# Weight units during attention: fixed steps behind the bias additions in place of every sixth slot

## The chip, the cores and the metric

The kernel runs on one core of one Trainium2 chip. The metric is the device time of one execution in microseconds (us). Five engines work side by side, each on its own queue and in the order of that queue: TensorE (PE, with its weight loads listed as PEld), VectorE (DVE), ScalarE (ACT), GpSimd (POOL) and SyncE (SP, which here only issues DMAs).

## The reference

Attention with a bias made by a small network, and behind it two feed-forward blocks, all in float32:

```python
# q, k, v: (4, 8, 576, 64); hidden 32
scores = scale * np.matmul(q, k.transpose(0, 1, 3, 2))
x = (psi_rel / psi_i)[..., None]           # log distances of positions
bias = np.maximum(x @ w1 + b1, 0.0) @ w2   # per head, the same for every batch
scores = scores + bias - max;  attn = exp(scores) / sum;  out = attn @ v
# 2304 tokens, 512 wide
h = x @ w_in                               # 512 x 2048
g = h * np.clip(h + 3.0, 0.0, 6.0) / 6.0
x = g @ w_out                              # 2048 x 512
gate = 1 / (1 + np.exp(-(x @ w_gate)));  val = x @ w_val    # 512 x 1536
y = (gate * val) @ w_out2                  # 1536 x 512
```

## The kernel before

A short first stage computes the bias and stores it in DRAM (about 57 us). Attention follows (to about 335 us), then the first feed-forward block (to about 750 us) and the second (to the end).

**Attention.** Two heads of one batch make a head unit; there are 16 (`NU`), numbered 0 to 15 here, and each is cut into nine steps (`NSTEP`), 0 to 8. Two steps in a row make a slot (`slot_of_two`, line 463), so an even head unit begins with a slot of its own, and an odd one shares its step 0 with step 8 of the unit before. A step is: score matmuls into a PSUM tile `s`, of which there are two (`scores`, line 342); the bias addition with a row minimum on DVE (line 346); the exponential on ACT, which also writes the row sum into `stat` (line 362); transposes of the probabilities on PE (line 400), copied out of PSUM by DVE or ACT (lines 390 and 392); and, some slots later, the products with v (lines 432 and 435) and their scaling on DVE (line 444). After steps 5 and 8 `invert` adds a constant to the row sums (line 368) and takes the reciprocal (line 369) on DVE. The q and k of the next head unit are split into a high and a low part by `prep`, in the main on POOL (lines 314 and 318); this work can begin when the last scores of the head unit before have been computed, since it overwrites their buffers.

**Weight units.** The weights of the feed-forward blocks come as 64-bit words and are turned into a high and a low float32 part, one block of 128 x 512 at a time: a weight unit. One weight unit is a DMA of the raw words (line 159, SP), an absolute value (line 175, ACT), a clamp (line 176, DVE), a shift (line 184, DVE), two merges with the raw words (lines 186 and 188, DVE), a rounding copy (line 192, ACT) and a subtraction (line 193, POOL). There are two buffers for raw words and three for the work tile `z`, each taken in the order in which the program asks for them. Ten weight units (`NPRE`) are made during attention by `whole`, which issues all eight instructions of a unit at the end of every sixth slot from slot 12 on (slots 12, 18, ... 66). Weight units 10 and 11 are begun by `tick` in slots 70 and 73 (`PRIME`), and the rest during the feed-forward blocks.

**What sets the order.** A scheduler orders each engine's queue ahead of time by a planned time for each instruction: whatever is ready goes in the order in which the program was written, and an instruction written later goes ahead when nothing written earlier is ready. `tc.issue_after(x)` adds an edge: what is written inside it for the engine of `x` is queued behind `x`, without a wait for its end; instructions for other engines are free. Before the change, the weight units stand behind `last_v`, the latest load of v, a DMA of SP: so their raw DMAs are queued behind it, and their DVE, ACT and POOL instructions are free. `PRIME`'s ticks have no such edge.

Of the kernel before, what the change touches and what calls it, by code (L numbers as in the profile page):

```python
# [10 lines left out]
F32 = mybir.dt.float32  # L11
F32R = mybir.dt.float32r
I32 = mybir.dt.int32
AF = mybir.ActivationFunctionType
ALU = mybir.AluOpType
# [3 lines left out]
P = 128  # L19
# [6 lines left out]
NSTEP = 9  # L26
# [18 lines left out]


NPRE = 10
EVERY = 6
PRIME = (NU * NSTEP // 2 - 2, NU * NSTEP // 2 + 1)
NALL = 19  # L50

# [45 lines left out]
def block_kernel(ctx: ExitStack, tc: tile.TileContext, q, k, v, mlp, w_in, w_out, w_gate, w_val, w_out2, dist_d,  # L97
                 rows_d, out):
    nc = tc.nc
# [24 lines left out]
    def ring(name):  # L124

        if name == "z":
            return stg.tile([P, 512], F32, name="z", bufs=3)
        return stg.tile([P, 2, 512], F32, name="raw", bufs=2)

    class Loader:  # L130
# [22 lines left out]
        def dma(self, i):  # L153
            if i < len(self.units) and self.units[i][1] is not None and i not in self.sent:
# [4 lines left out]
                nc.sync.dma_start(raw, self.units[i][1].bitcast(I32))  # L159
                self.sent.add(i)  # L160

        def magnitude(self, i):
            if i in self.raw:
                kind, _, to = self.units[i]
                raw = self.raw[i]
                if kind == "corner":
                    q, e, gv = to
                    if (e, gv) == (0, 0):
                        self.Z = moe.tile([P, 4, 2, 2 * P], F32, name="corners")
                    z = self.Z[:, 2 * e : 2 * e + 2, gv]  # L170
                    raw = raw.rearrange("p (k f) w -> p k f w", k=2)
                else:
                    z = ring("z")
                self.z[i] = (z, raw)
                nc.scalar.activation(z, raw[..., 1].bitcast(F32), AF.Abs)
                nc.vector.tensor_scalar(out=z, in0=z, scalar1=2.0**-15, scalar2=None, op0=ALU.max)

        def assemble(self, i):
            if i not in self.raw:
                return  # L180
            self.raw.pop(i)
            z, raw = self.z[i]
            zi = z.bitcast(I32)
            nc.vector.tensor_scalar(out=zi, in0=zi, scalar1=3, scalar2=0x3FFFFFF8, op0=ALU.logical_shift_left,
                                    op1=ALU.bitwise_and)
            nc.vector.scalar_tensor_tensor(out=zi, in0=raw[..., 1], scalar=-0x40000000, in1=zi,  # L186
                                           op0=ALU.bitwise_and, op1=ALU.bitwise_or)
            nc.vector.scalar_tensor_tensor(out=zi, in0=raw[..., 0], scalar=29, in1=zi,
                                           op0=ALU.logical_shift_right, op1=ALU.bitwise_or)

        def halve(self, z, slot, eng):
            nc.scalar.copy(slot[:, 0], z)  # L192
# [5 lines left out]
        def stage(self, z, idx):  # L198
            hl = self.pair()
            self.halve(z, hl, nc.gpsimd)  # L200
            nc.sync.dma_start(w_d[idx], hl.bitcast(F32))
            self.staged.add(idx)
# [23 lines left out]
                self.mix(to[1], to[2])  # L226
            self.done = i + 1

        def whole(self):
            i = self.n  # L230
            for stage in (self.dma, self.magnitude, self.assemble):
                stage(i)
            self.finish(i, nc.gpsimd)
            self.n += 1

        def tick(self):
            i = self.n
# [24 lines left out]
    load = Loader()  # L262

    attn = ExitStack()
    apool = attn.enter_context(tc.tile_pool(name="apool", bufs=1))
# [11 lines left out]
    Ks = [apool.tile([P, 2, 2, S], F32R, name=f"k{i}") for i in range(2)]  # L277
    Pm = [apool.tile([P, S + 64], F32, name=f"pm{i}") for i in range(2)]
    ident = apool.tile([P, P], F32, name="ident")
    stat = apool.tile([P, 5, NSTEP], F32, name="stat")  # L280
    low, sums = [stat[:, i] for i in range(2)], [stat[:, i] for i in range(2, 5)]
    spread = apool.tile([P, 5 * P], F32, name="spread")
    inv = apool.tile([P, S], F32, name="inv")
    w1c, b1c, w2bd = mlpc[:, 0:1], mlpc[:, 1:3], mlpc[:, 3:35]
# [44 lines left out]
    pts, us, avs, last_u, last_s = {}, {}, {}, [None], [None]  # L329
# [119 lines left out]
    last_v = [None]  # L449
# [3 lines left out]
    for n in range(NU):  # L453
        i = (NSTEP * n + 5) // 2 + 2
# [51 lines left out]
    with ExitStack():  # L506
# [20 lines left out]
        for i in range(2):  # L527
# [5 lines left out]
                                op1=ALU.mult)  # L533
# [30 lines left out]
        for G in range(NG):  # L564
            hid = [hids[(4 * G + ct) % 12] for ct in range(4)]
            nd = max(S - 16 * G, 16 * G + 16)
            for ct in range(4):
# [3 lines left out]
                else:  # L571
                    nc.vector.tensor_scalar(out=hid[ct][:, 0:nd], in0=tbl[:, 0:nd], scalar1=bpsi[:, 1, qd : qd + 1],  # L572
                                            scalar2=None, op0=ALU.max)
# [23 lines left out]
        def split_x(t, cs=range(4)):  # L597
            for c in cs:
                XH, XL = XS[t % 2][:, 0, c], XS[t % 2][:, 1, c]
                nc.scalar.copy(XH, tok(t)[c])  # L600
                eng = nc.gpsimd if 1 in XS else nc.vector
                eng.tensor_tensor(out=XL, in0=tok(t)[c], in1=XH.bitcast(F32), op=ALU.subtract)
# [21 lines left out]
        for i in range(NSLOT):  # L624
            slot_of_two(i)
            if i == NS // 2:
                w = keep.tile([P, 8 * TW], F32R, name="early")
                XS[0] = w.rearrange("p (r c t) -> p r c t", r=2, c=4)
                split_x(0)
            if i in (NS // 2 + 1, NS // 2 + 2):  # L630
                f = len(begun)
                begun[f] = hardswish(ring("z")[:, 0:TW], project(0, slots[2 * f], pp.tile([P, 2, 512], F32, name="s")[:, 0]))
            if i % EVERY == 0 and i > 10 and load.n < NPRE:
                with tc.issue_after(last_v[0].ins):
                    load.whole()
            if i in PRIME:
                load.tick()

        attn.close()
        moe = ctx.enter_context(tc.tile_pool(name="moe", bufs=1, reuse_waits="tile"))  # L640
# [225 lines left out]
        for v, (p, j) in enumerate(visits):  # L866
# [9 lines left out]
            for n in range(2):  # L876
                t = 2 * j + n
                os = bank(n)[0:NB]
                sums = [fp.tile([P, DM], F32, name="sum", bufs=4) for _ in range(NB)]
# [46 lines left out]
```

## Time and profile before

| | us |
|---|---|
| median of 3 runs | 1159.1 (1158.35 to 1160.71) |
| the profiled execution: its own time | 1160.52 |
| the profiled execution: its span in the trace | 1158.7 |
| PE busy | 1135.9 (98%) |
| DVE busy | 772.8 (67%) |
| ACT busy | 588.4 (51%) |
| POOL busy | 422.6 (36%) |

The span is the time from the first instruction to the last one's end. A busy share is an average over the stages. A matmul's end is modelled in the trace, so gaps on PE below some tenths of a microsecond are not seen in its busy time, and the length of a repeated stretch says more.

### The profile page before, as it was taken

To read this page: it belongs to the slowest core of one execution; us is meant where nothing else is said; L and a number is where in the kernel's file an instruction comes from. 1 tells how busy PE (TensorE), PEld (TensorE's weight loads), DVE (VectorE), ACT (ScalarE), POOL (GpSimd) and SP (SyncE) were. 2 spreads that over 40 slices of the span, in tenths; PEclk is the share of its full clock that TensorE was granted. 3 is DMA by queue.
4 is the path that set the end of the run, shared out by engine and by line. 5 is a ranking of instruction groups with operands and counts; after the bars stand their busy time and mean duration, and the time that the engine had idled before them with its cause. 6 is when DMAs were issued, how large, how long until landed. Compare 5 with 4: busy or idle time off the path is not lost.

```text
span 1158.7 us, 19146 instructions
## 1 busy us (share of the span) xinstructions
PE 1135.9 (98%) x6862; PEld 1012.2 (87%) x6862; DVE 772.8 (67%) x1495; ACT 588.4 (51%) x1296; POOL 422.6 (36%) x342
## 2 busy tenths in 40 slices
PE   8799999999999999999999999999999999999998
PEld 3277777777779999999999999999899898998997
DVE  8977878788868887355386775585367655644443
ACT  7988887877855545454455454342333222221221
POOL 0154544544316433232347445261333223311211
PEclk9999999999999999999999999999999999999999
DMA  6854436353213665249467759976878848757532
GB/s 203 298 162 110 158 95 183 112 165 103 78 55 110 209 218 200 101 174 340 167 228 255 253 189 357 395 261 251 308 254 309 311 165 299 285 181 258 191 109 73
DMA packets 83183, 236.82 MB, mean 204 GB/s; under 512 B 9616, under 2 KB 12304, under 8 KB 83088
## 3 DMA queue, kind: packets, MB, share of 16 engines
q1 hardware_dynamic: 83088, 235.60, 58.6%
q8 instruction: 54, 0.88, 0.3%
q14 instruction: 41, 0.34, 0.1%
HBM read 154.15 MB, written 81.41 MB: 203 GB/s over the span
## 4 chain that ended last, share of the span: by engine, by line
PE 84%; DVE 6%; ACT 2%; DMA 2%; issue 1%; POOL 1%; SPq 0%; POOLq 0%; DVEq 0%; ACTq 0%
PE o L673 17%; PE h L807 10%; PE o L807 10%; PE s L342 6%; PE o L862 6%; PE h L862 5%; PE h L611 5%; PE h L610 5%; PE h L612 5%; PE av L432 5%; PE tr L400 4%; PE av L435 1%; DVE z L186 1%; DVE u L346 1%; PE tr L379 1%
## 5 line engine op out<-in xcount | busy, mean ns | idle before, releaser
L673 PE MATMUL o<-gh,slot 128*128 128x384 f32 x768 | 196.0, 336 | 1.8 <-DVE take L392 1.8
L673 PEld LDWEIGHTS o<-gh,slot 128*128 128x128 f32 x768 | 139.2, 188 | 2.3 <-DVE take L392 2.1
L673 PE MATMUL o<-gl,slot 128*128 128x384 f32 x384 | 129.1, 336 | 0.7 <-DVE gl L659 0.7
L362 ACT ACTIVATE p<-u,stat 128x576 f32<-128x576 f32 x128 | 98.7, 773 | 29.2 <-DVE stat L346 28.4
L342 PE MATMUL s<-k,q 128*128 128x288 f32 x640 | 111.0, 309 | 0.7 <-ACT ptm L557 0.4
L346 DVE CUSTOM_DVE_ANT_0 u<-s,bias 128x576 f32<-128x576 f32 x128 | 93.6, 753 | 24.4 <-PE s L342 23.2
L843 POOL TENSOR_TENSOR gp<-s,gp 128x384 fp32r<-128x384 f32 x36 | 39.4, 1107 | 177.0 <-ACT gp L842 92.6
L617 DVE SCALAR_TENSOR_TENSOR g<-g,h 128x384 f32<-128x384 f32 x94 | 51.6, 549 | 70.2 <-ACT g L616 70.1
L659 DVE TENSOR_TENSOR gl<-g,gh 128x384 fp32r<-128x384 f32 x94 | 63.1, 671 | 48.3 <-ACT gh L658 45.8
L658 ACT CAST gh<-g 128x384 fp32r<-128x384 f32 x94 | 48.3, 513 | 91.6 <-DVE g L617 91.3
L193 POOL TENSOR_TENSOR hl<-corners,hl 128x512 fp32r<-128x512 f32 x42 | 57.2, 1366 | 94.3 <-ACT hl L192 79.3
L342 PEld LDWEIGHTS s<-k,q 128*128 128x128 f32 x640 | 88.8, 189 | 2.3 <-ACT ptm L557 0.6
L616 ACT ACTIVATE g<-h,half 128x384 f32<-128x384 f32 x94 | 54.3, 578 | 58.4 <-PE h L612 57.9
L807 PE MATMUL o<-x,slot 128*128 128x384 f32 x432 | 78.4, 336 | 1.4 <-DVE sum L787 1.4
L432 PE MATMUL av<-ptm,vn 128*64 128x288 f32 x512 | 77.8, 419 | 0.7 <-DVE x L444 0.7
L807 PE MATMUL h<-x,slot 128*128 128x384 f32 x432 | 77.8, 335 | 0.0
L807 PEld LDWEIGHTS o<-x,slot 128*128 128x128 f32 x432 | 75.1, 188 | 2.0 <-DVE sum L787 1.7
L807 PEld LDWEIGHTS h<-x,slot 128*128 128x128 f32 x432 | 75.2, 188 | 0.7
L400 PE MATMUL tr<-ident,p 128*128 128x128 f32 x512 | 72.2, 275 | 2.2 <-ACT inv L390 1.5
L673 PEld LDWEIGHTS o<-gl,slot 128*128 128x128 f32 x384 | 72.5, 189 | 1.3 <-DVE gl L659 1.3
L314 POOL TENSOR_TENSOR k<-early,one 128x576 fp32r<-128x576 f32 x30 | 34.4, 1167 | 106.3 <-DVE x L572 53.1
L843 POOL TENSOR_TENSOR x<-s,x 128x384 fp32r<-128x384 f32 x36 | 40.3, 1129 | 84.2 <-ACT x L842 50.5
(157 smaller groups left out, 2725.2 us busy)
## 6 DMA issues: line engine op xcount, KB each, us to landing
w<-hl SPq DMA_DIRECT2D x67, 512.0 KB, 3.3
slot<-w SPq DMA_DIRECT2D x67, 512.0 KB, 5.8
raw<-in_part_dram SPq DMA_DIRECT2D x50, 512.0 KB, 4.1
x<-xc SPq DMA_DIRECT2D x56, 384.0 KB, 6.0
sum<-sum SPq DMA_DIRECT2D x72, 256.0 KB, 3.5
early<-xc SPq DMA_DIRECT2D x28, 384.0 KB, 6.4
nbias<-ptm SPq DMA_DIRECT2D x36, 295.5 KB, 3.1
early<-in_part_dram SPq DMA_DIRECT2D x32, 288.0 KB, 4.3
```

The source lines that it names most:

```text
L342: last_s[0] = nc.tensor.matmul(ps[:, a, 0:HS], Q[:, q0 : q0 + P], K[:, r, h, HS * a : HS * a + HS], start=(i == 0), stop=(i == len(mm) - 1))
L346: last_u[0] = nc.vector.tensor_tensor_reduce(out=halves(u), in0=ps[:, :, 0:HS], in1=halves(bt), op0=ALU.add, op1=ALU.min, scale=-0.125, sc ...
L362: nc.scalar.activation(probs(t), us.pop(t), AF.Exp, bias=low[n % 2][:, s : s + 1], scale=-1.0, accum_out=sums[n % 3][:, s : s + 1])
L400: nc.tensor.transpose(ps[:, kc], pts[n, c][:, h, 64 * h + P * kc : 64 * h + P * kc + P], ident)
L432: nc.tensor.matmul(ps[64 * h : 64 * h + 64, 0:HS], vt[:, 4 * h + g], ptm[:, h, g, cols], start=(g == 0), stop=False)
L610: nc.tensor.matmul(ps[:, 0:TW], wh, XH[:, c], start=(c == 0), stop=False)
L611: nc.tensor.matmul(ps[:, 0:TW], wl, XH[:, c], start=False, stop=False)
L659: last_g[0] = nc.vector.tensor_tensor(out=gl, in0=g, in1=gh.bitcast(F32), op=ALU.subtract)
L673: nc.tensor.matmul(os[c][:, 0:TW], sl[:, r, P * c : P * c + P], x, start=(first and r == 0 and x is gh), stop=(last and x is gl))
L807: nc.tensor.matmul(ps[b], sl[:, r, o : o + P], x[:, c, s], start=(k < 4 and i == 0), stop=(i == len(mm) - 1), skip_group_check=True)
L843: nc.gpsimd.tensor_tensor(out=G[:, i, 1], in0=s, in1=G[:, i, 0].bitcast(F32), op=ALU.subtract)
L862: nc.tensor.matmul(os[i], x[:, P * i : P * i + P], slots[(base + 14 + e) % NALL][:, r], start=first, stop=last)
```

## The change

`whole` is replaced by `one_step`, which issues a weight unit in four parts, in four slots one after the other; weight unit m is made in head unit m + 2, for m from 0 to 9. Each part stands behind the latest load of v, as before, and also behind `last_u`, the bias addition of the second step of its slot, which is a DVE instruction. The condition gives these steps of the head unit for the four slots: in an even head unit 0 and 1 (raw DMA), 2 and 3 (absolute value), 4 and 5 (clamp, shift), 6 and 7 (merges, rounding copy, subtraction); in an odd one 8 of the unit before and 0, 1 and 2, 3 and 4, 5 and 6. The first part is in slot 9 and the last in slot 52, where it was slots 12 and 66. The number of instructions stays as it was. `PRIME` is unchanged. The second part of the change gives `stat` a last dimension of two and uses only its first word, so that row minima and row sums lie two words apart.

```diff
-EVERY = 6
+FIRST = 2
+        def absolute(self, i):
...
+            nc.scalar.activation(z, raw[..., 1].bitcast(F32), AF.Abs)
+        def clamp(self, i):
+            z = self.z[i][0]
+            nc.vector.tensor_scalar(out=z, in0=z, scalar1=2.0**-15, scalar2=None, op0=ALU.max)
+        def shift(self, i):
...
+        def merge(self, i):
...
-        def whole(self):
-            i = self.n
-            for stage in (self.dma, self.magnitude, self.assemble):
-                stage(i)
-            self.finish(i, nc.gpsimd)
-            self.n += 1
+        def one_step(self, i, at):
+            if at == 0:
+                self.dma(i)
+            elif at == 1:
+                self.absolute(i)
+            elif at == 2:
+                self.clamp(i)
+                self.shift(i)
+            else:
+                self.raw.pop(i)
+                self.merge(i)
+                self.finish(i, nc.gpsimd)
+                self.n = i + 1
...
-    stat = apool.tile([P, 5, NSTEP], F32, name="stat")
-    low, sums = [stat[:, i] for i in range(2)], [stat[:, i] for i in range(2, 5)]
+    stat = apool.tile([P, 5, NSTEP, 2], F32, name="stat")
+    low, sums = [stat[:, i, :, 0] for i in range(2)], [stat[:, i, :, 0] for i in range(2, 5)]
...
-            if i % EVERY == 0 and i > 10 and load.n < NPRE:
-                with tc.issue_after(last_v[0].ins):
-                    load.whole()
+            for m in range(NPRE):
+                at = i - (NSTEP * (m + FIRST) + 4) // 2 + 2
+                if 0 <= at <= 3:
+                    with tc.issue_after(last_v[0].ins), tc.issue_after(last_u[0].ins):
+                        load.one_step(m, at)
```

## Rows read from the trace of the kernel before

**Rows 1.** The page, part 1: busy time, share, instructions.

```profile
PE 1135.9 (98%) x6862; PEld 1012.2 (87%) x6862; DVE 772.8 (67%) x1495; ACT 588.4 (51%) x1296; POOL 422.6 (36%) x342
```

**Rows 2.** By stretch: length; PE, PEld, DVE, ACT, POOL busy; PEclk, DMA share, GB/s.

```profile
119.50:154.95 35.45, 34.53 (x256) 26.24 (x256) 29.57 (x73) 28.40 (x75) 18.54 (x15) 1.00 0.43 131
154.95:189.12 34.17, 34.17 (x256) 26.21 (x256) 25.83 (x72) 27.69 (x73) 17.22 (x14) 1.00 0.47 133
...
326.70:352.90 26.20, 25.37 (x150) 20.49 (x149) 18.36 (x29) 13.72 (x32) 9.39 (x7) 1.00 0.18 61
352.90:386.50 33.60, 31.81 (x172) 31.01 (x172) 29.46 (x49) 18.60 (x37) 16.93 (x11) 0.95 0.40 132
```

**Rows 3.** The same view, head units 4, 5, 6 and 7 alone.

```profile
119.50:136.74 17.24, 17.02 (x124) 12.76 (x125) 13.75 (x37) 14.28 (x39) 8.32 (x7) 1.00 0.49 152
136.74:154.95 18.21, 17.52 (x134) 13.48 (x131) 15.81 (x39) 14.12 (x37) 10.22 (x9) 1.00 0.37 112
154.95:171.88 16.93, 16.93 (x124) 12.72 (x125) 12.69 (x36) 14.52 (x40) 8.31 (x7) 1.00 0.27 74
171.88:189.12 17.24, 17.24 (x134) 13.48 (x131) 13.14 (x37) 13.17 (x35) 8.92 (x8) 1.00 0.66 191
```

**Rows 4.** Chain that ended last, head units 4 and 5: start, length, what.

```profile
126.52 1.83 DVE z L186
...
141.51 1.09 DVE z L176
```

**Rows 5.** POOL by time, head units 4 and 5: start, length, line, operation.

```profile
139.39 2.93 POOL L318 TENSOR_TENSOR q<-early,q 64x640 fp32r<-64x640 f32 x2
142.40 1.47 POOL L318 TENSOR_TENSOR k<-early,k 128x576 fp32r<-128x576 f32 x1
```

**Rows 6.** DVE by time, head units 6 and 7.

```profile
163.15 0.41 DVE L176 TENSOR_SCALAR z<-z 128x512 f32<-128x512 f32 x1
...
164.88 0.42 DVE L184 TENSOR_SCALAR z<-z 128x512 int32<-128x512 int32 x1
...
168.20 0.75 DVE L346 CUSTOM_DVE_ANT_0 u<-s,bias 128x576 f32<-128x576 f32 x1
...
171.20 0.76 DVE L346 CUSTOM_DVE_ANT_0 u<-s,bias_m 128x576 f32<-128x576 f32 x1 [0.92 <-PE s L342]
...
173.35 1.14 DVE L368 TENSOR_SCALAR stat<-stat 128x3 f32<-128x3 f32 x1 [0.70 <-ACT pm L362]
...
183.84 0.75 DVE L346 CUSTOM_DVE_ANT_0 u<-s,bias 128x576 f32<-128x576 f32 x1
...
184.94 0.52 DVE L444 TENSOR_TENSOR x<-av,inv 128x96 f32<-128x96 f32 x2 [0.35 <-PE av L435]
...
185.93 0.69 DVE L392 COPY ptm<-tr 128x512 f32<-128x512 f32 x1 [0.15 <-PE tr L400]
186.53 0.75 DVE L346 CUSTOM_DVE_ANT_0 u<-s,bias 128x576 f32<-128x576 f32 x1
...
187.51 0.76 DVE L346 CUSTOM_DVE_ANT_0 u<-s,bias_m 128x576 f32<-128x576 f32 x1 [0.22 <-PE s L342]
```

**Rows 7.** POOL by time, head units 6 and 7.

```profile
170.84 2.25 POOL L314 TENSOR_TENSOR k<-early,one 128x576 fp32r<-128x576 f32 x2 [1.17 <-PE s L342]
173.06 1.41 POOL L318 TENSOR_TENSOR k<-early,k 128x576 fp32r<-128x576 f32 x1
...
177.56 1.43 POOL L318 TENSOR_TENSOR k<-early,k 128x576 fp32r<-128x576 f32 x1
187.16 2.25 POOL L314 TENSOR_TENSOR k<-early,one 128x576 fp32r<-128x576 f32 x2 [8.17 <-PE s L342]
```

**Rows 8.** PE by time: score matmuls behind the ends of units 6 and 7.

```profile
174.40 1.31 PE L342 MATMUL s<-k,q 128*128 128x288 f32 x8
...
188.21 1.30 PE L342 MATMUL s<-k,q 128*128 128x288 f32 x8
```

**Rows 9.** SP and DVE by time: raw DMAs and weight unit 10, units 14 and 15.

```profile
290.38 16.86 SPq L159 DMA_DIRECT2D raw<-in_part_dram  x3
...
319.67 0.69 DVE L188 SCALAR_TENSOR_TENSOR z<-raw,z 128x512 int32<-128x512 int32 x1
```

More of the change, by code (lines that the diff above doesn't have):

```diff
@@ L160, in dma @@
                 self.sent.add(i)
+        def absolute(self, i):
+            kind, _, to = self.units[i]
+            raw = self.raw[i]
+            if kind == "corner":
+                q, e, gv = to
+                if (e, gv) == (0, 0):
+                    self.Z = moe.tile([P, 4, 2, 2 * P], F32, name="corners")
+                z = self.Z[:, 2 * e : 2 * e + 2, gv]
+                raw = raw.rearrange("p (k f) w -> p k f w", k=2)
+            else:
+                z = ring("z")
+            self.z[i] = (z, raw)
+            nc.scalar.activation(z, raw[..., 1].bitcast(F32), AF.Abs)
[3 more added lines that the diff above has]
+        def shift(self, i):
+            z = self.z[i][0].bitcast(I32)
+            nc.vector.tensor_scalar(out=z, in0=z, scalar1=3, scalar2=0x3FFFFFF8, op0=ALU.logical_shift_left,
+                                    op1=ALU.bitwise_and)
+        def merge(self, i):
+            z, raw = self.z[i]
+            z = z.bitcast(I32)
+            nc.vector.scalar_tensor_tensor(out=z, in0=raw[..., 1], scalar=-0x40000000, in1=z,
+                                           op0=ALU.bitwise_and, op1=ALU.bitwise_or)
+            nc.vector.scalar_tensor_tensor(out=z, in0=raw[..., 0], scalar=29, in1=z,
+                                           op0=ALU.logical_shift_right, op1=ALU.bitwise_or)
         def magnitude(self, i):
             if i in self.raw:
[L164 to L176, printed above, removed]
+                self.absolute(i)
+                self.clamp(i)
         def assemble(self, i):
@@ L181, in assemble @@
             self.raw.pop(i)
[L182 to L189, printed above, removed]
+            self.shift(i)
+            self.merge(i)
         def halve(self, z, slot, eng):
@@ L227, in finish @@
             self.done = i + 1
-        def whole(self):
-            i = self.n
-            for stage in (self.dma, self.magnitude, self.assemble):
-                stage(i)
-            self.finish(i, nc.gpsimd)
-            self.n += 1
+        def one_step(self, i, at):
+            if at == 0:
+                self.dma(i)
+            elif at == 1:
+                self.absolute(i)
+            elif at == 2:
+                self.clamp(i)
+                self.shift(i)
+            else:
+                self.raw.pop(i)
+                self.merge(i)
+                self.finish(i, nc.gpsimd)
+                self.n = i + 1
         def tick(self):
```

## The prediction, made before the changed kernel was run

> **What bounds the kernel now.** I read the busy times first: PE is busy 98% of the span, DVE 67% [rows 1]. So time can only come out of the stretches where PE stands still or the same work takes longer. The change touches attention, so I cut attention into pairs of head units (an even one and the odd one behind it), from one first bias addition to the next, and compared the pairs, which hold the same PE work (256 matmuls each) [rows 2]. They come in two kinds. Pair 6 and 7 takes 34.17 us with PE busy throughout; pairs 2 and 3, and 10 and 11, agree within 0.01. Pair 4 and 5 takes 35.45 with PE busy 34.53; pairs 8 and 9, and 12 and 13, agree within 0.01. The short kind makes one weight unit, in the second half of its even head unit; the long kind makes two, both in the first half of their head units. The loss is 35.45 - 34.17 = 1.28 us a pair, 3 x 1.28 = 3.84 us in all, and it can be split: the even unit takes 17.24 where 16.93 is possible (0.31), the odd one 18.21 where 17.24 is possible (0.97) [rows 3].
>
> The chain of waits says what the long pair waits for: the merge of line 186 at 126.52 (1.83 us in the chain) and the clamp of line 176 at 141.51 (1.09) [rows 4]. Elsewhere the same work is short: the clamp 0.41, the shift 0.42 [rows 6], a merge 0.69 [rows 9]. The difference is POOL. The stretched clamp stands beside `prep`'s two q operations of 139.39 to 142.32 [rows 5] and ends 0.3 us behind them (141.51 + 1.09 = 142.60). The row sum's addition at 173.35 takes 1.14 us and ends at 174.49, as POOL's k operation ends (173.06 + 1.41 = 174.47) [rows 6, 7]. So these DVE instructions stand until the POOL instruction in progress is over; bias additions and copies out of PSUM keep their length beside POOL.
>
> POOL is busy with `prep` from about step 8 of the unit before to step 3: in units 6 and 7 from 170.84 to 178.99, and again from 187.16 [rows 7]. Weight work is cheap behind step 3 and before step 8, and dear elsewhere.
>
> **The change, part by part.** The number of instructions stays the same; what moves is where a weight unit's five DVE and ACT places fall, and the pairs then have two weight units each in five pairs (head units 2 to 11).
>
> *The three long pairs.* Their early weight work goes: -3.84 us if nothing comes back.
>
> *Clamp and shift* go behind the bias addition of step 5 (even) or 4 (odd): 0.41 + 0.42 = 0.83 us. In the even unit 6 the shift stood in this place already, at 164.88, and the unit took its 16.93 us [rows 3, 6]. In an odd unit it is the time from 180.7 on, 1.7 us behind POOL's last `prep` operation [rows 7]; one more subtraction of a weight unit in POOL's queue (about 1.3 us, as long as its neighbours there) moves that to 180.3. I cost it at 0; if POOL ran later, a stall of at most one k operation, 1.43, would be in front of step 5's addition, which itself waits for PE.
>
> *Merges, even unit*: 2 x 0.69 = 1.38 us behind step 7's addition, which ends at 168.95. DVE has 0.92 us of idle time in front of step 8's addition alone [rows 6], so that addition is late by at most 0.5 us, unless the second merge runs into POOL's k operation at 170.84 and stands for up to 1.1. PE next wants that PSUM tile at the score matmuls of 174.40 [rows 8], 2.4 us behind the addition's end at 171.96. Both cases are covered: 0.
>
> *Merges, odd unit*: 1.38 us behind step 6's addition (end 184.59). The idle time that can take it is 0.35 in front of line 444, 0.15 in front of a copy and 0.22 in front of step 8's addition, 0.72 in all [rows 6], so that addition ends about 0.7 late, at 188.9. The score matmuls at 188.21 are eight, for two steps, in 1.30 us [rows 8]: the first four want step 7's tile (end 187.28 before, up to 0.9 late), the others, at about 188.7, step 8's tile. The margin is 0.9 and 0.5, so PE waits about 0.2 us. Bounds: 0 (the merges go into the gaps; no gain is possible where PE is busy throughout) and 0.97, the whole price of the disturbed odd unit. I take 0.2, what the margin leaves. Five odd units: +1.0 us. If the second merge slips behind step 7's addition, POOL has begun at 187.16 and it costs more (first rival).
>
> *What is behind the weight units in the queues.* On ACT the rounding copy stands in front of an exponential and the q copies; on POOL the subtraction stands among `prep`'s operations, which have until the end of the head unit. On SP a raw DMA is tied to the load of v as before, issued a head unit ahead, so the absolute value doesn't wait for it. Raw DMAs are 512 KB of a stage that has its DMA engines half busy [rows 2]. No cost.
>
> *Weight unit 10* is the one that changes without being in the diff. Its raw buffer comes free when weight unit 8 is merged. Before, its DMA went out right behind that of weight unit 9 at 290.38, and its last merge stood at 319.67 with its 0.69 us [rows 9]: `prep` was over, since there is no head unit 16. Now weight units 8 and 9 are made in head units 10 and 11, so unit 10, which has no edge, fills DVE's idle time in head unit 11 or 12, in the midst of `prep`. Bounds: 0 and 0.97. I take 0.4, between the even (0.31) and the middle price.
>
> *Row sums two words apart.* Only lines 368, 369 and 362 see it. The addition of line 368 stands 1.14 us in the undisturbed odd unit 7 [rows 6], and that unit still takes 17.24 with PE busy throughout [rows 3]. Whether it goes or stays: 0 by itself; in odd units it gives DVE 0.97 us in steps 0 to 3, where no weight work is left.
>
> That row shows a sum over 3 elements waiting for POOL like a clamp over 512. No row has such an operation on words apart, so the wait may as well stay; then an odd unit that takes over additions 0.5 late from the even one has 1.14 us of waiting in the same steps, and I count 0.03 of the first rival's chance for that. [...]
>
> *The sum*: -3.84 + 1.0 + 0.4 = -2.44 us. The profiled execution has 1160.5 us (span 1158.7 and 1.8 around it), so it would be 1158.1; it is 1.4 above the median of the runs, and from the median of 1159.1 it comes to 1156.6.
>
> **Rivals.** *The stall returns at the new place (slower).* In odd units the second merge is queued behind step 7's addition, where POOL has begun its k operations at 187.16. It stands there until 188.28, step 8's addition ends 1.4 late, past PE's margin of 0.5, and 0.97 is lost again, in five units, not three; the even ones lose 0.31 likewise. 5 x 1.28 = 6.4, and weight unit 10 a further 0.97: 6.4 + 0.97 - 3.84 = +3.5, so 1162.6; without the even ones +2.0, 1161.1. For it: the merge is the longest piece, and two weight units in a pair take DVE from 25.83 to about 28 of 34.17 us [rows 2]. Against: the merges are written ahead of the next slot's additions and are ready at once, so they go first. The point from which it decides is the start of line 188 in odd units against that of line 314.
>
> *Most is given back (no change).* The merges go first and delay the additions of steps 7 and 8 fully: 0.5 a unit, 2.5 in all, and 0.97 for weight unit 10: 3.84 - 3.5 = 0.3 gained, 1158.8.
>
> *The transition gains or loses too.* Behind attention PE lacks 0.83 us of 26.20 and 1.79 of 33.60, with a clock of 0.95 in the second stretch, which is 1.7 us more [rows 2]; there weight units 11 and on are late. Their start is tied to the last steps of attention in both kernels, so I expect the same picture, shifted. If this stretch happens to fall better, a gain of 3.84 and 1.0 of its 4.3 us gives 1154.3.
>
> *The ties do nothing*: if DVE's order came out as before, the long pairs would stay and 1159.1 with them. Five pairs with two weight units at other places make this unlikely; it counts with the no-change case.
>
> **How the numbers follow.** Forecast (a gain of 1.3 to 3.8, 1155.3 to 1157.8) 0.55; no change 0.23; the stall returns 0.12; transition 0.10. The range is 1154.0 to 1160.9: it leaves out most of the slower rival and little below. The likeliest case alone has 1155.3 to 1157.8. A measurement of this kernel can tell 0.2%, 2.3 us, from no change, so faster means below 1156.8: two thirds of the forecast's case (0.36), since 1156.6 and less is its nearer half, and the transition's 0.10, 0.46 in all. Slower means above 1161.4: 0.10 of the first rival. Within: the rest, 0.44.
>
> **What would show it.** In the trace after: the pairs of head units 4 and 5, 8 and 9, 12 and 13 at 34.2 to 34.5 us with PE busy throughout; clamp and shift at 0.41 to 0.43 in all ten weight units; merges at 0.69, in odd units in front of line 314; a long clamp or merge of weight unit 10 in head unit 11 or 12; all that is behind attention shifted by the same 2 to 3 us. The prediction is wrong if odd pairs stay above 35 us, if line 188 there is longer than 1 us, or if the stretch behind attention changes by more than a microsecond.

## The result, and the profile after

The changed kernel takes 1165.9 us (median of 5 runs, 1163.85 to 1166.64) against 1159.1 before: a ratio of 1.0054, 95% interval 1.0043 to 1.0066. It is slower by 0.5%, some 6.3 us by the ratio, where 1156.6 was forecast. The profiled execution took 1165.93 us, its span 1163.9. The page, part 1, answers to [rows 1]: PE's busy time is up by 4.6 us with the same 6862 matmuls, POOL's by 3.3, ACT's and DVE's by less than 2.

```profile
PE 1140.5 (98%) x6862; PEld 1013.3 (87%) x6862; DVE 773.8 (66%) x1495; ACT 590.2 (51%) x1296; POOL 425.9 (37%) x342
```

By stretch, as in [rows 2] (length; PE, PEld, DVE, ACT, POOL busy; PEclk, DMA share, GB/s): head units 2 to 13 together, pairs 4 and 5, 6 and 7, and two stretches behind attention.

```profile
84.94:299.22 214.28, 211.16 (x1526) 158.37 (x1526) 171.94 (x436) 170.15 (x442) 109.39 (x83) 1.00 0.47 137
120.33:156.28 35.95, 35.33 (x256) 26.40 (x255) 28.95 (x73) 28.53 (x75) 18.50 (x15) 1.00 0.43 126
156.28:192.33 36.05, 35.39 (x256) 26.47 (x255) 29.08 (x75) 28.68 (x75) 18.53 (x15) 1.00 0.50 144
331.85:358.05 26.20, 25.31 (x150) 20.43 (x149) 18.29 (x28) 13.69 (x32) 9.33 (x7) 1.00 0.18 61
358.05:391.70 33.65, 31.84 (x174) 30.96 (x173) 29.50 (x49) 18.68 (x37) 16.93 (x11) 0.96 0.38 132
```

Head units 2 to 13 of the kernel before, the same view:

```profile
85.34:294.20 208.86, 206.05 (x1526) 157.32 (x1526) 166.78 (x427) 168.26 (x439) 107.31 (x82) 1.00 0.46 133
```

These twelve head units hold the whole loss of the profiled executions, 214.28 - 208.86 = 5.42 us; the two stretches behind attention are the ones of [rows 2], shifted by 5.2. All six pairs are now long, 34.90 us in the last and 35.39 to 36.05 in the others, where 34.17 is possible. And PE hardly waits more: of the 5.42 us, 5.1 are busy time for the same 1526 matmuls.

**What the turn looks like.** DVE at the end of head unit 7 and the start of 8 (start, length, line, operation, tiles):

```profile
187.60 0.68 DVE L188 SCALAR_TENSOR_TENSOR z<-raw,z 128x512 int32<-128x512 int32 x1
188.20 0.69 DVE L413 COPY ptm<-tr 128x512 f32<-128x512 f32 x1
188.80 0.69 DVE L190 SCALAR_TENSOR_TENSOR z<-raw,z 128x512 int32<-128x512 int32 x1
189.40 0.76 DVE L367 CUSTOM_DVE_ANT_0 u<-s,bias 128x576 f32<-128x576 f32 x1
...
190.07 0.76 DVE L367 CUSTOM_DVE_ANT_0 u<-s,bias_m 128x576 f32<-128x576 f32 x1
...
190.75 0.97 DVE L389 TENSOR_SCALAR stat<-stat 128x6 f32<-128x6 f32 x1
...
193.65 1.08 DVE L389 TENSOR_SCALAR stat<-stat 128x3 f32<-128x3 f32 x1
```

The merges (lines 188 and 190 here, 186 and 188 in the kernel before) take their 0.68 us and begin before POOL's first k operation, as forecast. But the additions of steps 7 and 8 (line 367) come behind them, and behind those the row sums' addition, which in the kernel before came right behind line 444 of [rows 6], and now runs into POOL's k operation (DVE in head unit 7 before; POOL in head unit 7 after):

```profile
185.38 0.16 DVE L368 TENSOR_SCALAR stat<-stat 128x6 f32<-128x6 f32 x1
```

```profile
189.44 2.26 POOL L335 TENSOR_TENSOR k<-early,one 128x576 fp32r<-128x576 f32 x2 [7.06 <-PE s L363]
```

The chain of waits at this turn (start, length, what; its first row is from head unit 4) runs over ACT:

```profile
129.95 1.61 PE av L453 x12
...
188.10 1.61 PE s L363 x12
...
189.78 0.73 ACT q L331
190.51 0.52 ACT slot L206
191.03 0.78 ACT p L383 x2
191.81 0.65 ACT pm L383
...
192.50 0.52 ACT spread L394
...
193.06 0.55 PE tr L400 x3
...
193.74 1.60 PE av L453 x10
```

The q copy has to wait for the last scores, which read what it overwrites; behind it stands the rounding copy (line 206), and behind both the exponentials of steps 7 and 8, the first of which could have started when its bias addition ended, at about 190.1. Meanwhile PE does what it can, in pieces (PE by time):

```profile
190.09 0.60 PE L421 MATMUL tr<-ident,p 128*128 128x128 f32 x4
190.62 0.70 PE L453 MATMUL av<-ptm,vn 128*64 128x288 f32 x2
191.25 1.33 PE L363 MATMUL s<-k,q 128*128 128x288 f32 x8
193.06 0.55 PE L400 MATMUL tr<-ident,spread 128*128 128x128 f32 x3 [0.48 <-ACT spread L394]
...
193.67 1.67 PE L453 MATMUL av<-ptm,vn 128*64 128x288 f32 x10
```

Twelve matmuls of the products with v in a row take 1.61 us (129.95 in the chain); two and ten take 0.63 (190.62 to 191.25) and 1.60 (193.74), 0.62 more. The reason is in how they begin. The program writes these products in twos, one for each head of the head unit (line 453), and a product is two matmuls in the trace (384 for 192). In the row of twelve two matmuls begin together; here the first begins alone (PE by time, from 129.80 to 130.10 and from 190.54 to 190.84):

```profile
129.88 0.46 PE L453 MATMUL av<-ptm,vn 128*64 128x288 f32 x2
```

```profile
190.62 0.46 PE L453 MATMUL av<-ptm,vn 128*64 128x288 f32 x1
```

By the program, the second head's probabilities are missing at that time (experiment 7 has the wait by name): DVE copies those of the first head out of PSUM, ACT those of the second (the even and odd entries of `PT_EVAC`). ACT's copy of this slot stands behind the q copy, the rounding copy and both exponentials, although the transposes (line 421) had ended by 190.7; in the kernel before it stood between the two exponentials (ACT by time, after and before):

```profile
192.92 0.58 ACT L411 COPY ptm<-tr 128x512 f32<-128x512 f32 x1
```

```profile
188.10 0.57 ACT L390 COPY ptm<-tr 128x512 f32<-128x512 f32 x1
```

So a wait can go where PE's idle time doesn't show it. Over head units 2 to 13, 20 of the 384 matmuls begin with no other one within 0.02 us of them, four at each of five turns; in the kernel before there are none. The products with v are busy for 60.6 us against 57.2, 0.17 us for each matmul that runs alone (PE by line: operation, count, busy us and mean ns, idle time; first after, then before).

```profile
L363 PE MATMUL s<-k,q 128*128 128x288 f32 x482 | 85.4, 311 | 1.0 <-DVE stat L367 1.0
L453 PE MATMUL av<-ptm,vn 128*64 128x288 f32 x384 | 60.6, 419 | 0.0
```

```profile
L342 PE MATMUL s<-k,q 128*128 128x288 f32 x482 | 83.9, 309 | 0.0
L432 PE MATMUL av<-ptm,vn 128*64 128x288 f32 x384 | 57.2, 419 | 0.7 <-DVE x L444 0.7
```

### The profile page after: what moved, and what is told of

It reads as the page before. It is cut to its first block, busy times and chain, and to the rows that moved or that the text cites. A ratio compares the mean times of both kernels' runs of the same rounds, so it can differ in the third digit from the quotient of the medians.

```text
span 1163.9 us, 19175 instructions
## 1 busy us (share of the span) xinstructions
PE 1140.5 (98%) x6862; PEld 1013.3 (87%) x6862; DVE 773.8 (66%) x1495; ACT 590.2 (51%) x1296; POOL 425.9 (37%) x342
## 4 chain that ended last, share of the span: by engine, by line
PE 81%; ACT 5%; DVE 5%; issue 2%; DMA 1%; POOL 1%; SPq 0%; DVEq 0%; ACTq 0%; POOLq 0%
PE o L696 17%; PE h L830 10%; PE o L830 10%; PE o L885 6%; PE h L885 5%; PE h L631 5%; PE h L632 5%; PE h L633 5%; PE s L363 5%; PE av L453 4%; PE tr L421 4%; ACT p L383 2%; PE av L456 1%; ACT q L331 1%; PE s L599 1%
## 5 line engine op out<-in xcount | busy, mean ns | idle before, releaser
L453 PE MATMUL av<-ptm,vn 128*64 128x288 f32 x512 | 81.0, 419 | 0.0
```

Of the source, the lines that this page charges most:

```text
L453: nc.tensor.matmul(ps[64 * h : 64 * h + 64, 0:HS], vt[:, 4 * h + g], ptm[:, h, g, cols], start=(g == 0), stop=False)
```

## The experiments

The theories, in the words of the expectations: *row sums* (their pushed addition is the loss), *ScalarE* (ACT's order at the turn), *VectorE* or *amount* (the merges' work delays the bias additions), *place* (where in the head unit they stand). All ratios are to the kernel before; "the stretch" is head units 2 to 13 of the profiled execution (after 214.28 us, before 208.86).

**1. Row sums one word apart again.**

```diff
-    stat = apool.tile([P, 5, NSTEP, 2], F32, name="stat")
+    stat = apool.tile([P, 5, NSTEP], F32, name="stat")
```

> The changed kernel with the row sums one word apart again, all else as changed. If the stride costs anything by itself, this run lies below 1165.9 us and the row-sum additions get shorter than the 1.24 us they took at the longest in the changed kernel. If the stride does nothing, 1165.9 within 1 us, and the additions wait as long as there (0.97 and 1.08 us in odd units, about 1.25 us in even ones).

1166.5 us, 1.006 (1.0046 to 1.0073), with the same waits, 0.96 and 1.07 us at the turn. The stride does nothing.

**2. No addition to the row sums, in the changed kernel and in the one before.**

```diff
-        nc.vector.tensor_scalar(out=r, in0=r, scalar1=1e-9, scalar2=None, op0=ALU.add)
```

> The changed kernel without the addition of 1e-9 to the row sums (this part of the computation is left out; the sums are at least 1). Theory 'row sums': the addition stands behind GpSimdE's k operation about 1.25 us in an even unit and 2.2 us in an odd one, on the chain reciprocal, spread, transposes; seven pairs lose 9.25 us to their waits, and without the addition most of the 6.3 us comes back: about 1160 us or less, pairs of units near 34.5 us. Theory 'ScalarE': the absolute value and the rounding copy in the chain of exponentials are the loss: 1165 us, pairs stay near 36 us. A third way: the reciprocal waits in the addition's place, and the time stays at 1165 to 1166 us with the wait in the reciprocal's row.

> The kernel before, without the addition of 1e-9 to the row sums (left out of the computation). Theory 'row sums': the additions wait 0.49 us in an even unit and 1.30 us in an odd one there, but pairs without a weight unit in their odd unit run at 34.17 us with these waits, so they are hidden and the time stays at 1159 us within 1 us; if the wait is on the chain there too, about 1 us a pair, 1152 us. If the reciprocal waits instead, 1159 us.

1164.7 us, 1.0046 (1.0034 to 1.0059), and for the kernel before 1158.6, 0.9995 (0.9986 to 1.0004). DVE lost some 3 us of work and waiting a pair, yet the pairs 4 and 5, and 6 and 7, took 71.88 us together with 511 matmuls, against 72.00 with 512 (each alone, 34.88 and 37.00, holds unequal work, 252 and 259 matmuls). The reciprocal did not wait in the addition's place: DVE's busy time in these four head units fell from 58.03 to 52.14 us, and in the first version of experiment 11, also without the addition, it took 0.19 us at 188.27, beside POOL's k operation of 187.12 to 189.37. The pushed addition is worth some 1 us of the 6.3, no more.

**3. Rounding copy and subtraction two slots later.**

```diff
-                self.finish(i, nc.gpsimd)
...
+                if at == 5:
+                    with tc.issue_after(last_u[0].ins):
+                        load.finish(m, nc.gpsimd)
```

> The changed kernel with the rounding copy (ScalarE) and the subtraction (GpSimdE) of each weight unit issued two slots later, at steps 2 to 3 of the next head unit; the merges stay. Theory 'ScalarE': the rounding copy of 0.62 us at step 8, ahead of the exponentials of steps 7 and 8, goes from the chain at the start of odd units, and with it up to 0.6 us of each of ten units: about 1160 to 1163 us. Theory 'row sums': the merges still push the addition into GpSimdE's operation, 1165 us. If the copy only hinders elsewhere, 1166 us or more.

1163.4 us, 1.0037 (1.0024 to 1.005): some of it. Both together (without the addition, and later):

> The changed kernel without the addition of 1e-9 to the row sums (left out) and with the rounding copy and the subtraction two slots later. Alone, the first took 1.3 us off and the second 2.5 us. If they are two parts of one pile of work, the sum or a little less: about 1162 us. If each was hidden by the other (two chains of nearly equal length), more than the sum: 1160 us or less. If both act on the same wait, 1163 us.

1161.5 us, 1.0027 (1.0017 to 1.0036), about the sum of the two.

**4. No merges, in all ten weight units and in the five of odd head units.**

```diff
-                self.merge(i)
+                if i % 2 == 0:
+                    self.merge(i)
```

(This is the second of the two runs; the first leaves out the call.)

> The changed kernel without the two merges of the ten weight units of attention (left out of the computation); absolute value, clamp, shift, rounding copy and subtraction stay at their places. Theory 'VectorE is full at the turn from an odd head unit to the even one': in the changed kernel VectorE works without a gap from 185.2 to 194.9 us, with 1.37 us of merges in it, and the score matmuls wait for bias additions there; without the merges the additions come 1.4 us earlier, GpSimdE's k operation no longer meets the row-sum addition of step 5, and pairs come back to 34.2 to 34.8 us: about 1158 to 1160 us. Theory 'ScalarE': the rounding copy and the q copy still stand ahead of the exponentials of steps 7 and 8, and 1163 us or more stays.

> The changed kernel without the merges of the five weight units in odd head units (left out of the computation); those in even head units stay. If the odd head units are the cost, as the prediction's sum had it (0.2 us each there, none in the even ones), the pairs come to 34.2 to 34.4 us and the time to 1158 to 1160 us, as without any merges. If even and odd share it, about 35.1 us and 1162 us.

1158.3 us, 0.9992 (0.9983 to 1.0), and 1158.9, 1.0 (0.9992 to 1.0009). The stretch and the pair 6 and 7, without any merges and without those in odd head units:

```profile
84.95:292.24 207.29, 205.91 (x1526) 157.75 (x1526) 156.23 (x415) 169.96 (x442) 108.67 (x83) 1.00 0.48 141
153.13:187.18 34.05, 34.05 (x256) 26.23 (x256) 25.67 (x71) 28.50 (x75) 18.52 (x15) 1.00 0.51 146
```

```profile
84.42:293.20 208.78, 207.78 (x1526) 158.14 (x1526) 159.86 (x426) 169.06 (x442) 109.39 (x83) 1.00 0.47 140
153.53:187.92 34.39, 34.32 (x256) 26.23 (x256) 26.57 (x74) 27.90 (x74) 18.50 (x15) 1.00 0.49 141
```

This decides the place: five pairs of merges in odd head units are worth 214.28 - 208.78 = 5.5 us, 1.1 each; those in even ones 208.78 - 207.29 = 1.5 us in all (2.2 in the first four pairs; in the fifth, weight unit 10 ran differently in the two runs). Absolute value, clamp, shift, rounding copy and subtraction at their new places cost nothing as long as the merges don't stand in front of the bias additions: without merges the first four pairs take 34.05 to 34.11 us. What is left of the stretch without merges, 207.29 - 6 x 34.17 = 2.3 us, stands behind them: in that run all of weight unit 10 ran in head unit 11, its clamp and shift stretched to 0.79 and 0.94 us, and that head unit took 19.14 us; pair 12 and 13 took 34.89. ACT at the turn of experiment 4's first run shows what the merges change: the exponentials go first and the q copy behind them, as in the kernel before (187.32, 188.56 and 189.48 there):

```profile
185.37 0.78 ACT L382 ACTIVATE p<-u,stat 128x576 f32<-128x576 f32 x1 [0.65 <-DVE stat L366]
...
186.15 0.56 ACT L410 COPY ptm<-tr 128x512 f32<-128x512 f32 x1
186.61 0.78 ACT L382 ACTIVATE pm<-u,stat 128x576 f32<-128x576 f32 x1
...
187.53 0.72 ACT L330 CAST q<-early 64x640 fp32r<-64x640 f32 x1
```

**5. No second merge in odd head units.**

```diff
-            nc.vector.scalar_tensor_tensor(out=z, in0=raw[..., 0], scalar=29, in1=z,
+            if i % 2 == 0 or i >= NPRE:
+                nc.vector.scalar_tensor_tensor(out=z, in0=raw[..., 0], scalar=29, in1=z,
...
```

> The changed kernel without the second of the two merges in odd head units (left out of the computation). Without both it took 1158.9 us, with both 1165.9. If each microsecond of VectorE work there costs a microsecond, half: 1162 to 1163 us. If an odd head unit has a slack that clamp, shift and one merge still fit into, 1159 to 1160 us, and the second merge is the one that tips it. If already the first one pushes the row-sum addition beside GpSimdE, 1164 us or more.

1162.5 us, 1.0029 (1.002 to 1.0038): half, so each part of that VectorE work counts.

**6. ScalarE at the turn: less work, and more.** The rounding copy left out; and the copy of step 6 in odd head units given to ACT.

```diff
+            if copy:
+                nc.scalar.copy(slot[:, 0], z)
...
-                self.halve(z, slots[to], eng)
+                self.halve(z, slots[to], eng, copy=i >= NPRE)
...
+        for j in range(NPRE):
+            nc.gpsimd.memset(slots[j][:, 0].bitcast(F32), 0.0)
...
-            evac(PT_EVAC[s], ptm[:, h, :, P * c : P * c + P], ps)
+            evac("A" if s == 6 and n in (3, 5, 7, 9, 11) else PT_EVAC[s], ptm[:, h, :, P * c : P * c + P], ps)
```

> The changed kernel without the rounding copy of the ten weight units on ScalarE (left out; the high halves are zeros that GpSimdE writes in the first stage), everything else as changed. Theory 'ScalarE': 0.6 us goes from the chain ahead of the exponentials of steps 7 and 8 in each of ten head units, and the time falls below 1161 us. Theory 'VectorE': its work at the turn stays the same and so does the time, 1164 us or more.

> The changed kernel with one copy out of PSUM (step 6, 0.69 us on VectorE, 0.57 us on ScalarE) moved from VectorE to ScalarE in the odd head units 3 to 11, where that copy stands between the two merges. Theory 'amount of VectorE work': half of the merges' 1.37 us is given back, 0.7 to 1 us in each of five pairs: 1161 to 1163 us. Theory 'ScalarE is the chain at the turn': it gets worse, 1167 us or more. Neither: 1166 us.

1162.9 us, 1.0041 (1.0028 to 1.0054), and 1168.9, 1.0083 (1.0071 to 1.0096). The first lies between the bounds of the two theories. Without the rounding copy the pairs 4 to 9 took 35.39, 34.96 and 35.61, though weight unit 10 then ran early in head unit 11 and took 2 us back. Also, with the zeros that stand in for it (4.72 us on POOL in the first stage), head unit 2 begins at 87.23 in place of 84.94; an estimate from these two starts puts the time at about 1160.6 us without that delay, which would be theory ScalarE's. Relieving DVE of 0.69 us at ACT's cost made the stretch longer by 3.1 us:

```profile
84.77:302.16 217.39, 214.70 (x1526) 159.32 (x1526) 172.56 (x430) 172.78 (x447) 109.43 (x83) 1.00 0.45 135
```

PE's idle time fell there, from 3.1 to 2.7 us; its products with v grew, from 60.6 to 64.1 us, with 40 matmuls alone in place of 20. By both runs, work on ACT at the turn is dear; that the merges on DVE set ACT late is experiment 4.

**7. Products with v kept together.**

```diff
         for t in steps(i):
-            scores(t)
+            with ExitStack() as behind:
+                if last_a[0] is not None:
+                    behind.enter_context(tc.issue_after(last_a[0].ins))
+                scores(t)
...
-            av(n, a, g)
+            with tc.issue_after(last_s[0].ins):
+                av(n, a, g)
```

(`last_a` is the latest product with v; `turn_inv` stands behind it in the same way. The theories name each product, not each matmul: "one and five" are two and ten matmuls.)

> The changed kernel with an order for TensorE alone: the products with v stand behind the scores of their slot, and the scores and the transposes of the reciprocals behind the latest products with v, so that no other matmul is put between the products of one group. Theory 'order on TensorE': over head units 2 to 13 TensorE is busy 211.16 us in the changed kernel and 206.05 in the one before with the same matmuls, 3.4 us of it in the products with v (60.6 against 57.2), where five groups are cut into one and five; at 0.68 us a cut, the busy time of the products goes back to 57.2 us and the time to about 1162.5 us, 1161 if the scores' 1.5 us come back too. Theory 'the cuts only fill a wait': TensorE waits instead for bias additions and copies, its idle time of 3.1 us in this stretch grows by as much, and 1165 us or more stays.

1167.7 us, 1.0069 (1.0055 to 1.0083): not faster. The products wait now, for a copy on ACT, 6.3 us in the stretch, and their busy time stays, since the first two still run alone. No other matmul stands between them and the ten, and they take as long as before (PE by line over the stretch; PE by time at the end of head unit 7):

```profile
L453 PE MATMUL av<-ptm,vn 128*64 128x288 f32 x384 | 60.6, 420 | 6.3 <-ACT ptm L411 6.3
```

```profile
192.40 0.70 PE L453 MATMUL av<-ptm,vn 128*64 128x288 f32 x2
194.27 1.67 PE L453 MATMUL av<-ptm,vn 128*64 128x288 f32 x10 [1.17 <-ACT ptm L411]
```

So it isn't the other matmuls in between that cost the 3.4 us of busy time, it is that the two heads' products no longer begin together; and the other matmuls only fill the wait for ACT's copy.

**8. The four parts without the tie behind the bias addition.**

```diff
-                    with tc.issue_after(last_v[0].ins), tc.issue_after(last_u[0].ins):
+                    with tc.issue_after(last_v[0].ins):
```

> The changed kernel with its four parts in the same slots, but without the tie behind the bias addition: only behind the load of v, as before. If the tie itself forces the merges to the crowded place, the scheduler now puts them into earlier gaps and the time falls to 1160 us or less. If the number of weight units in odd head units sets it, 1164 us or more, or worse where a clamp or merge meets GpSimdE's operations of the first steps again (the long pairs of before, 35.45 us in all five pairs: 1161 to 1163 us).

1161.8 us, 1.0024 (1.0014 to 1.0034). About the long pair of before is back in the five pairs with two weight units, 35.20 to 35.32 us, with clamp and shift beside POOL's q and k operations of 175.31 to 179.81 (pair 6 and 7; DVE by time in head unit 7):

```profile
155.61:190.89 35.28, 34.56 (x256) 26.23 (x256) 29.11 (x76) 28.47 (x75) 18.61 (x15) 1.00 0.51 154
```

```profile
177.32 1.21 DVE L178 TENSOR_SCALAR z<-z 128x512 f32<-128x512 f32 x1
...
179.15 0.94 DVE L182 TENSOR_SCALAR z<-z 128x512 int32<-128x512 int32 x1
```

So the 6.3 us have two parts: about 2.8 for five weight units in odd head units where three were, at the old price, and about 3.5 for the places that the tie gives (dearer for the merges, cheaper for clamp and shift).

**9. Merges in the third part**, with clamp and shift; and the same with each even head unit from 2 to 14 filled first.

```diff
             elif at == 2:
                 self.clamp(i)
                 self.shift(i)
+                self.raw.pop(i)
+                self.merge(i)
             else:
-                self.raw.pop(i)
-                self.merge(i)
                 self.finish(i, nc.gpsimd)
...
+IN_UNIT = (2, 3, 4, 6, 7, 8, 10, 11, 12, 14)
...
-                at = i - (NSTEP * (m + FIRST) + 4) // 2 + 2
+                at = i - (NSTEP * IN_UNIT[m] + 4) // 2 + 2
```

> The changed kernel with the merges in the third part, with clamp and shift (behind the bias addition of step 5 in even head units, of step 4 in odd ones); rounding copy and subtraction stay in the fourth part. Leaving the merges out had given pairs of 34.1 us, so the merges are the term. Theory 'place': in the middle of a head unit VectorE has gaps of 2.2 us (0.72, 0.66, 0.35, 0.15, 0.22 and some more behind step 4's addition in the undisturbed odd unit of before), GpSimdE is idle there, and the merges go in: pairs of 34.2 to 34.7 us, 1156 to 1160 us. Theory 'amount': 2.2 us of VectorE work per head unit is too much wherever it stands, pairs stay at 35.5 us or more and the time at 1163 us or more.

> As the first of these four (merges in the third part), with the ten weight units in head units 2, 3, 4, 6, 7, 8, 10, 11, 12 and 14: each even one from 2 to 14 and three odd ones, so that three pairs have two weight units and four have one. Theory 'place': the four pairs with one take 34.2 us, the three others 34.2 to 34.7; 1155.5 to 1158 us, the fastest so far. Theory 'amount': the three full pairs take 35.5 us or more and the time is 1159 us or more.

1165.6 us, 1.0066 (1.0052 to 1.008), and 1159.5, 1.0007 (0.9998 to 1.0016). Theory place had at most 1160 and 1158 us, so the middle of an odd head unit is no better. In the second, with the merges of head unit 7 at 181.43 and 183.47, the row sums' addition went behind step 8's bias addition again, beside POOL:

```profile
187.94 1.13 DVE L389 TENSOR_SCALAR stat<-stat 128x6 f32<-128x6 f32 x1
```

**10. Whole weight units, as before, but mostly in even head units.**

```diff
-EVERY = 6
+WHOLE = (3, 12, 21, 30, 39, 48, 57, 66, 68, 69)
...
-            if i % EVERY == 0 and i > 10 and load.n < NPRE:
+            if i in WHOLE:
```

> The kernel before, with its weight units made whole as there, but at the end of slots 12, 21, 30, 39, 48, 57 and 66 (steps 6 and 7 of the even head units 2 to 14, where its short pairs have them) and three more in slots 3, 68 and 69. Theory 'odd head units have no room for a weight unit': all pairs run at 34.2 us, 3.84 us less than before in the middle, minus what slots 3, 68 and 69 cost: 1155 to 1157 us. If it is two weight units a pair of whatever place that costs, the same, since no pair has two; if the loss moves to the end of attention, where three stand close together, 1159 us or more.

1157.3 us, 0.9993 (0.9983 to 1.0003), not clear of the kernel before. The pairs are all short (34.15 to 34.18 us, the last 34.55), but head units 0 and 15, which took the rest, grew from 9.76 and 15.57 us; head unit 0 also ran at a granted clock of 0.71, where it was 1.00 before (PE was busy 11.01 us for 64 matmuls there, before 9.35 for 68), so its growth is not the weight unit's alone (pair 6 and 7, head unit 0, the stretch from head unit 15's start):

```profile
157.00:191.17 34.17, 34.17 (x256) 26.21 (x256) 25.83 (x72) 27.69 (x73) 17.22 (x14) 1.00 0.47 135
59.14:70.97 11.83, 11.01 (x64) 10.71 (x65) 8.69 (x24) 9.47 (x23) 6.42 (x5) 0.71 0.70 202
311.02:328.05 17.03, 16.53 (x126) 12.55 (x123) 15.57 (x43) 13.06 (x34) 2.97 (x3) 1.00 0.29 99
```

**11. Towards a version that beats both.** The second version of 9 without the addition to the row sums; that with the copy of step 4 in head units 3, 7 and 11 on ACT; and that with the order of 7.

```diff
-        nc.vector.tensor_scalar(out=r, in0=r, scalar1=1e-9, scalar2=None, op0=ALU.add)
...
-            evac(PT_EVAC[s], ptm[:, h, :, P * c : P * c + P], ps)
+            evac("A" if s == 4 and n in (3, 7, 11) else PT_EVAC[s], ptm[:, h, :, P * c : P * c + P], ps)
```

> The version with merges in the third part and weight units in head units 2, 3, 4, 6, 7, 8, 10, 11, 12 and 14 (1159.5 us), without the addition of 1e-9 to the row sums (left out). There the addition of step 5 in odd head units stands behind step 8's bias addition, 1.13 us beside GpSimdE's k operation, and the bias addition behind it is late for TensorE. Theory 'a pushed row-sum addition is the price': the three full pairs fall from 35.1 and 34.8 by about 1 us each: 1156 to 1157.5 us. Theory 'amount of VectorE work': the addition's place is taken by another late piece and 1159 us stays.

> As the first of these four (no addition to the row sums), and the copy of step 4 in head units 3, 7 and 11 on ScalarE and not on VectorE, where it stands between the two merges. Theory 'amount': VectorE then has 1.5 us more there than in an odd head unit without a weight unit, and all pairs come to 34.2 to 34.4 us: 1154.5 to 1156.5 us, below both kernels. If ScalarE's exponentials are held up by the copy, no better than the first of the four.

> The same order for TensorE in the version with weight units in head units 2, 3, 4, 6, 7, 8, 10, 11, 12 and 14, merges in the third part, no addition to the row sums (left out) and the copy of step 4 of head units 3, 7 and 11 on ScalarE (1158.8 us; head units 2 to 13 take 207.8 us with TensorE busy throughout, products with v 59.2 us). Theory 'order on TensorE': three cuts less, 2.0 us, about 1156.8 us, 2 us below the kernel before. Theory 'the cuts only fill a wait': 1158.8 us or more, with TensorE idle in that stretch.

1161.3 us, 1.002 (1.0011 to 1.0028); 1158.8, 0.9994 (0.9985 to 1.0003); 1156.5, 0.998 (0.9971 to 0.9988). The first got slower with less work, which neither of its theories had: PE never waits, but its products with v are busy for 61.3 us against 59.2 with the addition, with 24 matmuls alone against 12, 0.17 us each again. The second missed its forecast of 1154.5 to 1156.5. A row sum is at least 1, so 1e-9 is lost in its rounding, and the addition can go for good. The last came out as its theory of the order on TensorE had it, and beats both kernels by a little, with PE busy throughout its stretch:

```profile
84.66:291.17 206.51, 206.42 (x1526) 158.64 (x1526) 151.07 (x401) 170.49 (x442) 107.53 (x82) 1.00 0.47 136
```

## Why the prediction was wrong

- *The three long pairs, -3.84*: right in its mechanism. No clamp or shift of the ten meets POOL any more; all take the short time forecast, the shift 0.41 to 0.43 us (line 182), and the clamp likewise (line 178 alone, its range in ns, count):

```profile
L178 DVE TENSOR_SCALAR z<-z x11: 412/423/424, 94.9 to 256.1; 128x512 f32<-128x512 f32 x11
```

- *Clamp and shift, 0*: right; experiment 4 has them at their places in pairs of 34.05 us.
- *Merges, even unit, 0*: too small; 1.5 us in all, 0.3 to 0.9 a pair in the first four.
- *Merges, odd unit, 0.2 each*: this is the step that failed. They cost 1.1 us each in the profiled executions (experiment 4), 5.5 us where 1.0 was summed. The forecast took DVE's gaps, 0.72 us, and PE's next use of the two PSUM tiles, and found a margin of 0.5 for the scores. It did not ask who else waits for the bias additions of steps 7 and 8: ACT's exponentials, and what stands behind them in ACT's queue.
- *What is behind the weight units in the queues, no cost*: wrong on ACT, and the other half of the same mistake. With the additions behind the merges, the q copy and the rounding copy come ahead of the exponentials of steps 7 and 8, ACT's copy for the second head comes behind all of them, and PE waits for it or runs the first head's product alone (experiments 6 and 7).
- *Weight unit 10, 0.4*: it ran in head units 11 and 12, with one merge of 1.65 us there; pair 12 and 13 took 34.90, 0.7 above the short one, but that includes the turn from head unit 11. Without merges in the ten, weight unit 10 ran elsewhere and the pair took 34.89 all the same (experiment 4), so what it costs here is not shown.
- *Row sums two words apart, 0*: right, and the waits stayed, which the prediction held possible without a row for it: over six words beside POOL's k operation the addition took 0.97 us two apart, and 0.96 one apart (experiment 1). In step 5's row of odd head units it grew, from 0.16 us at 185.38 to 0.97 at 190.75, which by experiment 2 is worth some 1 us.
- *The rivals*: the slower one named this place, and line 188 against POOL's k operation as the point that decides. That merge, line 190 here, came out in the forecast's favour (188.80 against 189.44), and it was slower all the same.
- *The signs*: of the three that would show the prediction wrong, one came, pairs above 35 us; the merge stayed at 0.69 us and the stretch behind attention kept its length.

The sum with the measured terms: the six pairs of head units 2 to 13 took 214.28 - 6 x 34.17 = 9.26 us more than short ones, 5.5 for the merges of odd head units, 1.5 for those of even ones and 2.3 that stay without them in head units 11 to 13. Before, they had taken 3.84 more; 9.26 - 3.84 = +5.4 in place of -2.4.

What stays open: why the planned order puts the q copy and the rounding copy ahead of the exponentials. That the planner takes them because the bias additions are late fits all runs, but no run changed ACT's order alone.

## What to carry to other kernels

A piece of work that goes into an engine's gaps need not be free, as the merges here were not (1.1 us for each pair of them in odd head units): list every engine that waits for the instructions behind it, and what its queue puts in front when they come late. And where a scheduler fixes the order by planned times, a delay can come back as another order on other engines, as 1.4 us of merges did here, so compare the engines' orders at the tightest turn, and PE's busy time for the same matmuls, before PE's idle time. Where a trace shows matmuls that begin together, look whether what feeds them comes at the same time: here each one that began alone took 0.17 us more of PE's busy time.

## What the runs showed of the hardware

- Matmuls of the products with v (128*64) began two at a time in the kernel before (all 384 of head units 2 to 13), and in the changed kernel 20 of 384 began alone, where the second head's copy was late: twelve in a row took 1.61 us, two alone 0.63 and the ten behind them 1.60, with other matmuls in between (changed kernel) or none (experiment 7). In five runs, 384 of them were busy for 57.2 us with none alone, 59.2 with 12, 60.6 with 20, 61.3 with 24 and 64.1 with 40, at the same granted clock (1.00).
- A one-source addition over 128 x 6 words stood 0.97 us beside a POOL operation with the words two apart and 0.96 with them one apart, at the same turn; the reciprocals of the row sums took 0.16 to 0.20 us in the changed kernel and the one before (32 in each), beside POOL too (0.18 us at 192.23, POOL's operation 191.65 to 193.08).
